# Retention attention and maxout FFN in one kernel: the first weights loaded ahead of block 2, and the first FFN product cut in two halves

## The chip, the cores and the metric

The kernel runs on one core of one Trainium2 chip. The metric is the device time of one execution in microseconds (us), from its first to its last instruction with the little that lies around them; smaller is better.

A core has five engines that run side by side, each through its own queue of instructions in order: TensorE (PE, matmuls; its weight loads are shown as PEld), VectorE (DVE), ScalarE (ACT), GpSimd (POOL) and SyncE (SP), whose queue here issues nearly all transfers. Engines wait for one another, and for transfers, by semaphores.

## The reference

```python
# q, k, v: (8 batches, 8 heads, 576 positions, 64), float32
scores = q @ k.T / sqrt(64)
gamma  = 1 - 2.0 ** (-5 - arange(8))                       # one per head
ret    = scores * where(i >= j, gamma ** (i - j), 0)       # causal, decaying with distance
x      = (ret @ v) -> rows (batch, position), columns (head, dim)   # 4608 x 512
h      = max(x @ w1, x @ w2, x @ w3)                       # w1, w2, w3: 512 x 768
out    = h @ w_out                                         # w_out: 768 x 512, out: 4608 x 512
```

The four weight matrices come as 64-bit floats. [...] the kernel reads them as pairs of 32-bit words and converts them to float32 itself.

## The kernel before

**Blocks.** The 4608 rows are cut into 36 blocks of 128 rows, and four blocks make one FFN tile of 512 rows. For a block the retention is worked out in this way: q and k are transposed on TensorE (`transposes`, L286) and copied from PSUM by ACT (L287); `scores` multiplies them (L300), and DVE multiplies the result with a causal mask into `st`; v is scaled by the decay of its position on POOL (`decay`, L253, giving `vd`); `state` forms k times v for the blocks that follow (`kv`, L366), and `keep` adds it up on DVE and POOL (L372 to L375); `values` multiplies scores and v (`o`, L405), adds the part that comes from the state (L418), and `output` has DVE scale the result into `xT`, the transposed input of the FFN, 128 columns of it for each block. Small DVE steps go through a helper and so stand at L198.

**FFN of the first tile.** Each of the three matrices has six pieces of 128 output columns, and `w_out` has six more; 24 pieces in all. `load_weights(n)` issues the next n pieces from SP, each piece of the three first matrices as two transfers of 256 KB (L502). Six pieces may be under way; a further one is loaded whenever a piece has been converted. `convert(n)` goes n steps further in the conversion of the pieces in their order. A piece takes on DVE two masks (L620, L625), a sum (L631) and two steps of the product (L636, L642, which gives `w`); on ACT one step `mant` (L621) and two steps `expo` (L623, L626). `up_plain` multiplies a piece with the 512 columns of `xT` (L736): four pairs of matmuls. The first result of a piece of columns is copied by ACT (L741), the later ones are combined by a maximum on DVE (L740). For the first product of all, the columns are split in 384 and 128, so that it may begin before block 3's columns are there.

**Order.** Each engine executes in the order in which the program text issues, and this is written out by hand. SP's queue before: k, q, v of block 0; of block 1; state factors `gs`; k, q, v of block 2; k, q of block 3; piece 1; v of block 3; piece 2; k, q, v of block 4; pieces 3 to 6. TensorE's queue before: transposes 0, scores 0, transposes 1, state 0, values 0, scores 1, transposes 2, state 1, values 1, transposes 3, scores 2 and 3, state 2, values 2, values 3 with state 3, then the first FFN product, transposes 4 and the second product. The conversion of piece 1 stands around `values([2])`, that of piece 2 behind `values([3])`. Then `ffn(0)` begins, and the generator `steps(1)` places the retention of blocks 4 to 7 between its products. Later tiles use products with fewer multiplications (L693 to L713); the change leaves them alone.

Of the kernel before, what the change touches and what calls it, by code (L numbers as in the profile page):

```python
# [48 lines left out]
C = 128  # L49
NT = 4 * C  # L50
NH = NT // 2
# [30 lines left out]
def kernel(  # L82
# [23 lines left out]
    CPT = NT // C  # L106
# [68 lines left out]
    def half(j):  # L175
        return slice(D * j, D * (j + 1))
# [5 lines left out]
    late, chores, urgent, scaling, spread = {}, deque(), deque(), deque(), []  # L182
# [42 lines left out]
            vas[g, c] = vpool.tile([P, H, D], FP32, tag=f"va{c}", name=f"va{c}")  # L225
        return vas[g, c]

    def load(g):
        if g >= BY_PE and ("q", g) not in raws:
            load_blocks(g, *range(C // 32))  # L230
        for n, src in (("k", k), ("q", q), ("v", v)) if g < BY_PE else (("k", k), ("v", v)):
            if n == "v" and g == CPT - 1:
                load_weights(1)
            if n == "v" and g >= BY_CHUNKS:
                for c in range(2):
                    b, pos = divmod(g * C + D * c, S)
                    nc.sync.dma_start(stacked(g, c)[half(c)], v[b, :, pos:pos + D, :].rearrange("h p d -> p h d"))
                continue
            bufs = {"k": 3, "q": 2, "v": 4}[n]
            pool, bufs = (raw0, 1) if n != "v" and g < BY_PE and g % (bufs + 1) == bufs else (raw, bufs)  # L240
            if n == "v":
                t = vpool.tile([C, H, D], FP32, tag="va0", name="vraw")
            else:
                t = pool.tile([C, H, D], FP32, tag=n, name=n + "raw", bufs=bufs)
            raws[n, g] = t
            for row, b, pos, m in spans(g):
                nc.sync.dma_start(t[row:row + m], src[b, :, pos:pos + m, :].rearrange("h p d -> p h d"))  # L247
# [19 lines left out]
    def transposes(g):  # L267
        both = qks[g] = {}
        if g >= BY_CHUNKS:
            for n, tag in (("k", "kT"), ("q", "m1")):  # L270
                both[n] = att.tile([P, H, D], FP32, tag=tag, name=tag, bufs=2 if n == "k" else 3)
            ms[g, 0], ms[g, 1] = att.tile([P, H, D], FP32, tag="m0", name="m0"), both["q"]
        else:
            for n in ("k", "q"):
                tag, bufs = ("kT", 2) if n == "k" else (f"m{g % 2}", 3)
                both[n] = att.tile([P, NP, C], FP32, tag=tag, name=n + "T", bufs=bufs)
        if g >= BY_PE:
            for n in ("k", "q"):
                soon(partial(nc.vector.transpose, both[n][:].rearrange("a p c -> a (p c)"),
                             raws.pop(("kx" if n == "k" else n, g))[:].rearrange("a x y i -> a (x y i)")))  # L280
            return
        for n, src in (("k", raws["k", g]), ("q", raws.pop(("q", g)))):
            pool, tag = (ps_r, "r") if g >= CPT else (ps_x, "x")
            pt = pool.tile([P, NP, C], FP32, tag=tag, name=n + "t")
            for p in range(NP):
                nc.tensor.transpose(pt[:, p, :], pair(src, p), ident[:C, :C])  # L286
            nc.scalar.copy(both[n][:], pt[:])  # L287
# [95 lines left out]
    def head(c, n):  # L383

        return NP * c + n
# [104 lines left out]
    def load_weights(n):  # L490
        for _ in range(n):
            if not to_load:
                return
            i, fb = piece = to_load.popleft()
            t = bits[piece] = wraw.tile([P, DM], I64, tag="bits", name="bits")
            if i == "out":
                nc.sync.dma_start(t[:], moe_w_out[fb * P:(fb + 1) * P, :])
            else:
                heads = WS[i][:, fb * P:(fb + 1) * P].rearrange("(h p) f -> p h f", p=D)
                blocks = t[:].rearrange("p (n f) -> p n f", f=P)  # L500
                for c in range(2):
                    nc.sync.dma_start(blocks[half(c)], heads[:, head(c, 0):head(c, NP)])  # L502
# [177 lines left out]
    def convert(n):  # L680
        for _ in range(n):
            next(converting, None)
# [48 lines left out]
    def up_plain(t, h, fb, i):  # L731
        ps = (ps_x, ps_y)[fb % 2].tile([P, NT], FP32, tag="xy"[fb % 2], name="up")
        first_of_all = t == 0 and (fb, i) == (0, 0)
        for cols in (slice(0, NT - C), slice(NT - C, NT)) if first_of_all else (slice(0, NT),):
            for dc in range(NDC):
                nc.tensor.matmul(ps[:, cols], lhsT=w_sb[i, fb][:, dc * P:(dc + 1) * P], rhs=xT[t][:, dc, cols],  # L736
                                 start=dc == 0 and cols.start == 0, stop=dc == NDC - 1,
                                 skip_group_check=first_of_all)
        if i > 0:
            return lambda: nc.vector.tensor_tensor(h[:, fb, :], h[:, fb, :], ps[:], op=ALU.max)  # L740
        return lambda: nc.scalar.copy(h[:, fb, :], ps[:])  # L741

    def ffn(t):

        h = hpool.tile([P, NF, NT], FP32, tag="h", name="h")
        if t == 0:
            for fp, i in units:
                for fb in (2 * fp, 2 * fp + 1):
                    maximum = up_plain(t, h, fb, i)
                    if CPT not in qks:  # L750
                        maximum()
                        transposes(CPT)
                        convert(4)
                        continue
                    convert(4)
                    maximum()
                yield
            convert(6)
            for fb, _ in enumerate(downs_plain(t, h)):
                convert(4 if fb < 2 else 4 * len(pieces))  # L760
                if fb == 2:
                    while_converting.close()
                    late["pool"] = ctx.enter_context(tc.tile_pool(name="late", bufs=1))
                    late_room()
                    sums_of_outs()
                elif fb > 2:
                    chore({3: 4, 4: 0, 5: 2}[fb])
                if fb in (1, 3):
                    yield
            yield  # L770
            return
        if t == 1:
            spread.append(True)
            weight_sums(0)
            weight_sums(2)
        plain = (2, 3) if t == 1 else ()
        order = (2, 3, 0, 1, 4, 5) if t == 1 else (0, 1, 4, 5, 2, 3)
        total = sum(24 if fb in plain else len(PRODUCTS) for fb in order)
        count = parts = 0
        for n, fb in enumerate(order):  # L780
            if fb not in plain:
                while fb // 2 not in summed_fp:
                    chore()
            steps_of_one = up_plain_all(t, h, fb) if fb in plain else up(t, h, fb)
            for step, cost in enumerate(steps_of_one):
                if fb in plain:
                    chore(4 if (fb, step) == (plain[-1], 1) else 8)
                elif step % 2 and (step % 4 == 1 or t == 1 or len(urgent) > 6) or t == 1 and step % 5 == 4:
                    chore(len(urgent) > 0)
                elif step % 4 == 2 and chores:  # L790
                    chores.popleft()()
                if step % 3 == 2:
                    scale()
                count += cost or 1
                if count * (NF // 2 * 3) >= (parts + 1) * total:
                    parts += 1
                    yield
            if n % 2:
                sums_of_hidden(h, fb // 2)
                if fb in plain:  # L800
                    weight_sums(fb // 2)
        chore(len(urgent))
        for n, _ in enumerate(downs(t, h)):
            chore(4)
            scale(2)
            if n in (1, 3):
                yield
        yield
# [8 lines left out]
    for g in range(CPT):  # L817
        load(g)
        if g == 1:
            for j in range(2):  # L820
                nc.sync.dma_start(gs[half(j)], state_decay[half(j), :, half(j)])
    load_weights(1)
    load(CPT)
    load_weights(4)
    decay(0)
    key_masks()
    transposes(0)
# [9 lines left out]
    keep(0)  # L837
    scores(1)
    first_output()
    transposes(2)  # L840
    state_factors()
    decay(2)
    state(1)
    keep(1)
    values([1], [1])
    transposes(3)
    decay(3)
    scores(2)
    scores(3)
    state(2)  # L850
    keep(2)
    convert(2)
    values([2], [2])
    convert(2)
    values([3], [3])
    convert(4)
    keep(3)
    decay(CPT)
    convert(2)

    def steps(t):

# [97 lines left out]
```

## Time and profile before

| | us |
|---|---|
| median of 7 runs | 769.5 |
| lowest and highest | 767.25, 771.82 |
| the profiled execution | 770.87 |
| its span, first to last instruction | 768.9 |

| engine | busy us | share of the span |
|---|---|---|
| PE | 751.3 | 98% |
| PEld | 606.1 | 79% |
| DVE | 588.9 | 77% |
| ACT | 388.9 | 51% |
| POOL | 91.7 | 12% |

The mean granted TensorE clock is 0.998 of full speed. In a row of the profile, `w<-mant,expo` gives what is written and read, `x16` a number of instructions, and "idle before <-releaser" how long the engine stood still ahead of them and what ended it. A busy TensorE is not one at its peak, since matmuls overlap and their ends are modelled; distances from start to start say more.

### The profile page before, as it was taken

The page shows a single profiled execution, that of the slowest core. Times are in us where ns is not written, and L with a number is a line of the kernel's source. Part 1 is how long each engine was busy: PE and PEld are TensorE (multiplying, and loading weights), DVE is VectorE, ACT ScalarE, POOL GpSimd, SP SyncE. Part 2 cuts the span into 40 slices and gives each one's busy share as a digit, 9 for nine tenths or more (in the row PEclk, how much of TensorE's full clock was granted, in tenths as well). Part 3 has the DMA queues.
Part 4 walks back from the last instruction along what each step waited for, and adds up shares of the span by engine and source line. Part 5 has one row for each costly group of instructions (what it writes and reads, how often), then busy time and mean ns, then how long its engine had stood idle before and what let it go on. Part 6 is the DMA issues. An engine that isn't in the chain of part 4 may idle for free.

```text
span 768.9 us, 16109 instructions
## 1 busy us (share of the span) xinstructions
PE 751.3 (98%) x5928; PEld 606.1 (79%) x5928; DVE 588.9 (77%) x1268; ACT 388.9 (51%) x1057; POOL 91.7 (12%) x112
## 2 busy tenths in 40 slices
PE   8999999998999999999999999999999999999998
PEld 7645544686888888888888888878888888888887
DVE  2998998888676867788688959775888678855672
ACT  3574641364256644664466446653666256514651
POOL 3210022102010110011011102010101001100000
PEclk9999999999999999999999999999999999999999
DMA  9995762414041414232243324142415141001001
GB/s 222 221 234 128 186 140 79 87 27 86 28 101 39 79 47 103 51 69 58 68 84 59 66 60 93 30 82 62 80 39 98 42 87 39 2 15 41 1 1 55
DMA packets 230319, 59.40 MB, mean 77 GB/s; under 512 B 211168, under 2 KB 228960, under 8 KB 230240
## 3 DMA queue, kind: packets, MB, share of 16 engines
q1 hardware_dynamic: 229664, 58.04, 35.1%
q8 instruction: 46, 0.75, 0.4%
q10 hardware_dynamic: 576, 0.33, 0.1%
q14 instruction: 33, 0.27, 0.1%
HBM read 48.89 MB, written 9.44 MB: 76 GB/s over the span
## 4 chain that ended last, share of the span: by engine, by line
PE 86%; DVE 9%; SPq 2%; issue 1%; DMA 1%; ACT 1%; DVEq 0%
PE a L713 15%; PE b L713 13%; PE dx L553 11%; PE up L736 11%; PE c L713 6%; PE dz L553 5%; PE d L713 5%; PE e L713 4%; PE o L436 4%; DVE part L693 4%; PE down L723 3%; PE dy L553 3%; DVE m L325 2%; PE sk L317 2%; SPq L247 1%
## 5 line engine op out<-in xcount | busy, mean ns | idle before, releaser
L693 DVE TENSOR_TENSOR part<-part 128x256 f32<-128x256 f32 x460 | 208.3, 462 | 68.7 <-ACT part L698 60.5
L698 ACT COPY part<-a 128x256 f32<-128x256 f32 x276 | 101.8, 369 | 64.6 <-PE a L713 58.6
L698 ACT COPY part<-b 128x256 f32<-128x256 f32 x230 | 85.6, 372 | 86.0 <-PE b L713 81.7
L736 PE MATMUL up<-xT,w 128*128 128x512 f32 (+2 forms) x200 | 84.7, 578 | 1.6 <-DVE w L642 1.6
L713 PE MATMUL a<-s,w 128*128 128x256 f32 x276 | 82.9, 382 | 2.5 <-ACT part L698 2.5
L713 PE MATMUL b<-s,n 128*128 128x256 f32 x276 | 82.1, 379 | 0.0
L736 PEld LDWEIGHTS up<-xT,w 128*128 128x128 f32 x200 | 36.8, 190 | 43.6 <-issue 38.9
L186 ACT ACTIVATE kraw<-kraw,gk 128x64 f32<-128x64 f32 x208 | 66.9, 349 | 0.3
L713 PE MATMUL d<-s,w 128*128 128x256 f32 x184 | 56.7, 390 | 5.4 <-DVE part L693 5.4
L713 PEld LDWEIGHTS a<-s,w 128*128 128x128 f32 x276 | 51.5, 190 | 11.9 <-ACT part L698 3.9
L713 PEld LDWEIGHTS b<-s,n 128*128 128x128 f32 x276 | 52.4, 190 | 7.1
L335 POOL TENSOR_TENSOR va<-va,gs_of 64x512 f32<-64x512 f32 x24 | 26.3, 1097 | 261.7 <-DVE va L333 159.7
L713 PE MATMUL b<-xT,n 128*128 128x256 f32 x184 | 57.3, 394 | 0.0
L713 PE MATMUL c<-xT,w 128*128 128x256 f32 x184 | 54.7, 379 | 0.0
L713 PE MATMUL a<-xT,n 128*128 128x256 f32 x184 | 47.3, 380 | 0.3 <-ACT part L698 0.3
L713 PE MATMUL e<-xT,w 128*128 128x256 f32 x184 | 47.2, 379 | 0.0
L693 DVE TENSOR_TENSOR h<-part 128x256 f32<-128x256 f32 x92 | 40.6, 442 | 6.9
L713 PEld LDWEIGHTS d<-s,w 128*128 128x128 f32 x184 | 34.2, 191 | 14.5 <-DVE part L693 10.1
L325 DVE TENSOR_TENSOR m<-sk,gm 64x512 f32<-64x512 f32 x56 | 38.5, 688 | 8.4 <-PE sk L321 7.2
L553 PE MATMUL dx<-To,H 128*128 128x256 f32 (+1 forms) x204 | 44.9, 370 | 0.0
L560 ACT COPY part<-dx 128x256 f32<-128x256 f32 (+1 forms) x34 | 10.5, 362 | 63.4 <-PE dx L553 61.2
L530 POOL TENSOR_TENSOR H<-h,H 128x256 f32<-128x256 f32 x24 | 18.9, 788 | 188.0 <-DVE H L529 149.0
(121 smaller groups left out, 1372.5 us busy)
## 6 DMA issues: line engine op xcount, KB each, us to landing
bits<-in_moe_w_dram SPq DMA_DIRECT2D x36, 256.0 KB, 5.3
out_dram<-osb SPq DMA_DIRECT2D x35, 256.0 KB, 2.1
kraw<-in_k_dram SPq DMA_DIRECT2D x32, 256.0 KB, 3.1
qraw<-in_q_dram SPq DMA_DIRECT2D x224, 32.0 KB, 2.1
kxraw<-in_k_dram SPq DMA_DIRECT2D x224, 32.0 KB, 2.1
va<-in_v_dram SPq DMA_DIRECT2D x56, 128.0 KB, 3.1
bits<-in_moe_w_out_dram SPq DMA_DIRECT2D x6, 512.0 KB, 6.6
vraw<-in_v_dram SPq DMA_DIRECT2D x7, 256.0 KB, 5.2
```

The lines of the kernel that those rows point to most:

```text
L186: scaling.popleft()()
L317: nc.tensor.matmul(sk[c][half(c), h, :], lhsT=kr[half(c), h, :], rhs=vas[g, c][half(c), h, :], start=True, stop=True)
L325: nc.vector.tensor_tensor(ms[g, c][half(c)], sk[1 - c][half(c)], gm[half(c)], op=ALU.mult)
L335: nc.gpsimd.tensor_tensor(to[half(1)], to[half(1)], gs_of[half(1)].unsqueeze(2).to_broadcast([D, H, D]), op=ALU.mult)
L436: nc.tensor.matmul(o[half(c), n % 2, n // 2, half(m)], lhsT=vas[g, m][:, h, :], rhs=ms[g, m][:, h, :], start=m == 0 and n == 0, stop=True, ...
L530: urgent.append(lambda: (pool(s3, a11, a21, op=ALU.subtract), pool(s4, a12, s2, op=ALU.subtract)))
L553: nc.tensor.matmul(o, lhsT=hS[n](fp)[:, m * P:(m + 1) * P], rhs=late["T"][n][:, fp, cols], start=first and fp == 0 and (m == 0 or last and ...
L693: nc.vector.tensor_tensor(out, a, b, op=op)
L698: nc.scalar.copy(t[:], ps[step[0]][:])
L713: nc.tensor.matmul(ps[chain][:], lhsT=factor(w, fb), rhs=xS[t][x], start=n == 1, stop=ends, skip_group_check=True)
L723: nc.tensor.matmul(b[:], lhsT=h[:, fb, m * P:(m + 1) * P], rhs=w_sb["out", fb], start=(fb == 0), stop=(fb == NF - 1))
L736: nc.tensor.matmul(ps[:, cols], lhsT=w_sb[i, fb][:, dc * P:(dc + 1) * P], rhs=xT[t][:, dc, cols], start=dc == 0 and cols.start == 0, stop= ...
```

## The change

Three things are done. **Loads:** SP's queue gets piece 1 behind the state factors, ahead of block 2, and no longer inside block 3; piece 2 comes behind block 3's v; piece 3 goes between q and v of block 4; then v of block 4 and pieces 4 to 6. **Conversion:** the first two steps of piece 1 go ahead of `values([1])`, the last two behind it; the first two of piece 2 go behind `keep(2)`, its last two behind the copy of the first product's result; `decay(4)` moves there too, and the six steps that follow are those of pieces 3 and 4 that came in part earlier. **First product:** its columns are split in 256 and 256. The first half (blocks 0 and 1) comes behind the transposes of block 3; then `meanwhile` issues scores 3, state 2, keep 2, values 2, values 3 and keep 3; then comes the second half. State 1 moves ahead of the transposes of block 2, scores 2 ahead of those of block 3.

```diff
-    def load(g):
+    def load(g, names="kqv"):
...
-            if n == "v" and g == CPT - 1:
-                load_weights(1)
+            if n not in names:
+                continue
...
-        for cols in (slice(0, NT - C), slice(NT - C, NT)) if first_of_all else (slice(0, NT),):
+        for cols in (slice(0, NH), slice(NH, NT)) if first_of_all else (slice(0, NT),):
+            if cols.start > 0:
+                late.pop("meanwhile")()
...
                     if CPT not in qks:
                         maximum()
+                        convert(2)
+                        decay(CPT)
                         transposes(CPT)
-                        convert(4)
+                        convert(6)
                         continue
...
         if g == 1:
             for j in range(2):
                 nc.sync.dma_start(gs[half(j)], state_decay[half(j), :, half(j)])
+            load_weights(1)
     load_weights(1)
-    load(CPT)
-    load_weights(4)
+    load(CPT, "kq")
+    load_weights(1)
+    load(CPT, "v")
+    load_weights(3)
...
     first_output()
+    state(1)
     transposes(2)
     state_factors()
     decay(2)
-    state(1)
     keep(1)
-    values([1], [1])
+    convert(2)
+    values([1], [])
+    convert(2)
+    scores(2)
     transposes(3)
     decay(3)
-    scores(2)
-    scores(3)
-    state(2)
-    keep(2)
-    convert(2)
-    values([2], [2])
-    convert(2)
-    values([3], [3])
-    convert(4)
-    keep(3)
-    decay(CPT)
-    convert(2)
+
+    def meanwhile():
+        scores(3)
+        state(2)
+        keep(2)
+        convert(2)
+        values([2], [])
+        values([3], [3])
+        keep(3)
+
+    late["meanwhile"] = meanwhile
```

Constants: `C` = 128, `NT` = 512, `NH` = 256, `CPT` = 4.

## The prediction

> **What bounds the kernel now.** I read the page's busy table first, then TensorE's waits, then the timeline of the first 31 us, because everything the change touches happens there.
>
> ```profile
> PE 751.3 (98%) x5928; PEld 606.1 (79%) x5928; DVE 588.9 (77%) x1268; ACT 388.9 (51%) x1057; POOL 91.7 (12%) x112
> ```
>
> TensorE stands still for only about 17 us of 768.9. The start takes 1.4 of them (warm-up matmuls fill the rest until the first block arrives at 4 us); the largest single stall, 3.6 us on DVE, is at 183 us, far from the change. TensorE's waits between 11 and 27 us, which are what the change can fill (columns: us in all, times, longest):
>
> ```profile
> PE up L736 <- DVE w L642: 1.6, 1, 1.6
> PE qt L286 <- DMA qraw<-in_q_dram: 1.4, 2, 1.2
> PE kt L286 <- DMA kraw<-in_k_dram: 0.6, 1, 0.6
> PE o L405 <- POOL vd L253: 0.3, 1, 0.3
> ```
>
> They sum to 3.9 us. In the timeline (start, length, what, idle before it) the places are seen:
>
> ```profile
> 12.24 0.63 PE L286 MATMUL kt<-ident,kraw 128*128 128x128 f32 x4 [0.62 <-DMA kraw<-in_k_dram]
> 13.10 0.63 PE L286 MATMUL qt<-ident,qraw 128*128 128x128 f32 x4 [0.23 <-DMA qraw<-in_q_dram]
> ...
> 17.59 0.63 PE L286 MATMUL qt<-ident,qraw 128*128 128x128 f32 x4 [1.19 <-DMA qraw<-in_q_dram]
> 18.14 2.06 PE L300 MATMUL s<-qT,kT 64*128 64x128 f32 x32
> ...
> 26.37 3.74 PE L736 MATMUL up<-xT,w 128*128 128x384 f32 x16 [1.61 <-DVE w L642]
> 29.95 0.60 PE L286 MATMUL kt<-ident,kraw 128*128 128x128 f32 x4
> 30.39 0.60 PE L286 MATMUL qt<-ident,qraw 128*128 128x128 f32 x4
> 30.82 3.60 PE L736 MATMUL up<-xT,w 128*128 128x512 f32 x8
> ```
>
> The second product starts at 30.82, and from there to 110 us the stage table shows TensorE busy all the time. So **the measure of the change is when that second product starts**; a shift there is passed on whole. DMA is full as well: in this table of stages the last two numbers are the share of the 16 engines and GB/s.
>
> ```profile
> 8.00:12.00 4.00, 3.62 (x56) 2.97 (x55) 1.65 (x4) 1.12 (x2) 2.66 (x3) 1.00 1.14 264
> 12.00:16.00 4.00, 3.53 (x58) 2.84 (x59) 2.50 (x7) 1.56 (x4) 1.73 (x2) 1.00 1.07 246
> ```
>
> Whatever goes to the front of SP's queue therefore pushes what was there.
>
> **What the Trainium skill says.** "TensorE: Matmul & The Clock Gate", on engine queue depths, says ACT and DVE are strict FIFO. The trace agrees: the first product's result is there at about 30.0, and ACT copies it at 32.37, behind two steps of the third piece (30.99 and 31.74) that stand ahead in its queue. "DMA: Bandwidth & Descriptors", section on why a DMA increments its semaphore by 16, says a transfer is spread over up to 16 engines and has landed only when the last has finished. The trace agrees: of the packets between 16 and 17 us only 33 of 283 are of the small kind of q, k and v, so block 3's q was all but moved, yet its transposes start at 17.59. "TensorE: Matmul & The Clock Gate", Part 1, also says that after about 3.4 us idle TensorE's clock is halved. The trace agrees at 183 us: 3.62 us of stall, then a window at 0.55 of the clock:
>
> ```profile
> 183.45:187.07 3.62, 0.00 (x0) 0.00 (x0) 3.42 (x7) 0.42 (x2) 2.01 (x3) 1.00 0.59 128
> 187.07:190.50 3.43, 3.43 (x9) 2.77 (x10) 2.65 (x7) 0.99 (x3) 0.36 (x1) 0.55 0.16 37
> ```
>
> **Part 1: the first piece moves ahead of block 2 on SP.** The piece is two issues of 256 KB (12.90 to 14.65 on SP) that now come before 7.97. Block 2's k landed at 7.97 + 4.1 = 12.1, its q at 8.62 + 4.3 = 12.9, each time confirmed by the transposes 0.1 to 0.2 us later. 524 KB at 250 GB/s are 2.1 us. To this I add a lag: small packets ahead of the piece were late in landing. Block 3's q, next to the piece before, was moved by about 16.0 and landed at 12.13 + 5.3 = 17.4, a lag of 1.4, where k and q of block 2 lag about 0.8; so 0.6 more. q of block 2 then lands at 12.9 + 2.7 = **15.6**. Lower end: v of block 1 landed at 10.45 and q of block 2 2.45 us later, with 2.5 transfers of 256 KB (the state factors count half), 0.98 each; two more make 14.9. Upper end: from k of block 3 (15.0) to v of block 3 (21.4) four transfers, with the piece among them, took 6.4, or 1.6 each; 10.45 + 4.5 x 1.6 = 17.6.
>
> From v of block 3 on the bytes are as before. On SP, two issues of the third piece now precede v of block 4: it lands about 2 us after its 26.3, and its only user, the scaling on POOL (1.22), is wanted by the kv product at 35.4: covered. The eighth piece goes behind block 5's k, q, v, whose buffers are free; before, its conversion came at 46.6 on DVE, and I place its landing at 44.5 (block 5's last issue ends at 39.6 now, two issues or 1.3 us earlier then, and 6.2 to land), still covered. Block 5 lands earlier, which buys nothing: its transposes at 43.03 did not wait.
>
> **Part 2: the conversion of the first piece.** It goes into DVE time that was idle, but its chain hangs on block 2: ACT's queue has both copies of block 2 and the two small factor copies ahead. Measured offsets: q landing 12.92 to the end of the factor copies 14.83, 1.9; on ACT 0.79 + 0.76 + 0.72 = 2.3; on DVE 0.71 + 0.74 = 1.5 to the first matmul. So the first half product starts at 15.6 + 5.7 = **21.3**. TensorE meanwhile does block 2's transposes, block 1's output, scores of block 2 and transposes of block 3, done by about 19.8: it waits 1.5 us for weights again. Scores of block 2 used to run with those of 3, now earlier, and their mask multiply on DVE sits behind the conversion (done by 22.7, wanted at 25).
>
> **Part 3: two halves with blocks 2 and 3 between.** A 256-column pair of matmuls takes 0.43 in the later product rows, so a half is 4 x 0.43 = 1.73 and both 3.46; the old split at 384 took 3.58 (26.37 to 29.95), a gain of 0.1. After the first half, by starts in the timeline: scores of block 3 1.02, kv 0.49, output 2 1.00 + 0.60, output 3 0.93, kv 0.56, state part 0.67: 5.3. They end at 21.3 + 1.7 + 5.3 = 28.3. The second half needs all of block 3's columns, a **new wait**: first of two DVE multiplies, 0.46. Before, 384 columns ran beneath it. The half ends at 28.3 + 0.46 + 1.73 = 30.5, block 4's transposes (0.87) at 31.4. The second piece's last steps are on DVE behind the multiplies: from 28.3, 0.8 + state 0.35 + 0.6 + 0.71 + 0.74 = 3.2, so weights at **31.5**.
>
> The sum: second product at 31.5 against 30.82, **0.7 us later**. As waits: k and q of block 2 grow from 0.85 to about 2.9; 1.19 and 0.28 go; the weights' 1.6 becomes 1.5; 0.46 and 0.1 are new. What was moved is given back, because the transfer ahead delays the block on which its own conversion waits.
>
> Costed at nothing: the third piece's steps on ACT now stand behind the first result's copy and block 4's copies; I get its weights at 36.1 and their use at 36.7, a cover of 0.5, and what exceeds it is paid in full. The scaling of block 4 on POOL moves behind the first result and keeps 4 us. DVE, about 98% busy from 30 to 60, then holds its lead over TensorE, as both shift alike.
>
> The profiled execution took 770.87 (span 768.9), 1.4 over the median 769.5. I predict 769.5 + 0.7 = **770.2**; 0.2%, about what a measurement of this kernel can tell from no change, is 1.5 us.
>
> **The rivals.** *Gain:* block 2 is not delayed, the piece being taken up by slack in DMA. Then q lands at 12.9, the second product starts at 28.8: 767.5. Against it: a share above 1 and 264 GB/s in the stage where the piece would go. Even my lower end of 14.9 only brings zero. A further gain could come from the stall at 183 us and its half clock, if the new alignment shortens it; nothing speaks for that.
> *Slower, block 2 behind the piece:* transfers around it land at 1.6 each, q at 17.6, second product 33.5, +2.7: 772.2. For it: v of block 3 behind the same piece did so. Against it: there the second piece pressed from behind too. It decides from q later than 16.4.
> *Slower, clock:* TensorE stands still from 12.4 until k of block 2 at about 14.8. If that halves the clock for one window of 3.4 us, 1.7 us are lost, of which the 1.5 of waiting for weights hide most: +0.2 to +1.5 over the forecast. The stall of 3.62 brought it on, that of 1.61 did not.
> *Nothing:* the path runs elsewhere and the move doesn't show: 769.5.
>
> **How the numbers follow.** Forecast 0.52 and nothing 0.04, both within 0.2%: same 0.56. Block 2 late 0.26 and clock at its worst 0.07: slower 0.33. Gain 0.11: faster. The range goes from 768.4 (between the gain and no change) to 772.5 (just beyond the late block 2); about one in ten lies outside at each end. The forecast's own range is 769.5 to 771.0 (q at 14.9 to 16.4).
>
> **What would show it.** Right: transposes of block 2 wait over 2 us for k, the half product starts near 21.3 after a wait on DVE's w, a wait of about 0.5 on xT ahead of the second half, second product near 31.5. Wrong: block 2's q landing near 13 (gain) or beyond 16.4; a granted clock below 1 before 20 us; a stall on DVE's w between 31 and 60; a changed stall at 183.

## The result and the profile after

The changed kernel takes 774.89 us (median of 12 runs, 772.10 to 776.39), the kernel before 769.83 (31 runs). The ratio is 1.0064, 95% interval 1.0053 to 1.0075: slower by some 5 us. The forecast was 770.2 with a range to 772.5, so the result lies outside it, on the side to which it gave 0.33. The profiled execution took 776.32 (span 774.5).

The busy table of the changed kernel shows 3.6 us more of busy TensorE for the same instructions, the first hint that some of them ran slower:

```profile
PE 754.9 (97%) x5928; PEld 608.2 (79%) x5928; DVE 588.7 (76%) x1268; ACT 388.9 (50%) x1057; POOL 92.2 (12%) x112
```

TensorE's waits between 11 and 36 us, changed kernel:

```profile
PE kt L286 <- DMA kraw<-in_k_dram: 2.9, 1, 2.9
PE up L738 <- ACT mant L621: 1.5, 1, 1.5
PE up L738 <- DVE w L642: 1.0, 1, 1.0
PE up L738 <- DVE xT L198: 0.5, 1, 0.5
PE qt L286 <- DMA qraw<-in_q_dram: 0.2, 1, 0.2
```

They sum to 6.1 where 3.9 stood before. In this profile the second product is 4.0 later than in the first one of the kernel before (34.87 against 30.82): 2.2 of it are these waits, and about 1.7 is TensorE at half its clock, as shown next. The wait put down to ACT's `mant` is one for the first weights: `mant` was done long ago (17.75 to 18.51), and the matmul starts 0.15 us after DVE has written `w`. The same stretch in the timeline of the changed kernel:

```profile
15.12 0.63 PE L286 MATMUL kt<-ident,kraw 128*128 128x128 f32 x4 [2.87 <-DMA kraw<-in_k_dram]
15.95 0.66 PE L286 MATMUL qt<-ident,qraw 128*128 128x128 f32 x4 [0.21 <-DMA qraw<-in_q_dram]
16.54 1.98 PE L405 MATMUL o<-st,vd 128*64 128x128 f32 x16
18.45 1.13 PE L418 MATMUL o<-qT,state 64*64 64x128 f32 x16
...
23.29 1.97 PE L738 MATMUL up<-xT,w 128*128 128x256 f32 x8 [1.46 <-ACT mant L621]
...
31.03 1.99 PE L738 MATMUL up<-xT,w 128*128 128x256 f32 x8 [0.51 <-DVE xT L198]
...
34.87 3.70 PE L738 MATMUL up<-xT,w 128*128 128x512 f32 x8 [0.97 <-DVE w L642]
```

The second product starts at 34.87 instead of 30.82. Block 1's output (L405, 16.54 to 18.45) takes 1.91 us from start to start; it took 0.97 before. The stage table of the changed kernel says why: the third number from the end is the granted clock.

```profile
12.00:16.00 4.00, 0.92 (x15) 0.60 (x10) 2.61 (x7) 0.16 (x1) 0.00 (x0) 1.00 0.96 205
16.41:19.83 3.42, 3.42 (x36) 2.63 (x36) 0.22 (x1) 3.04 (x7) 1.74 (x2) 0.50 1.08 264
```

TensorE was busy 0.92 of 4 us, and after that it had half its clock for 3.42 us, so some 1.7 us of work were lost. What follows on DVE decides how much of that comes through. DVE's queue in the changed kernel, around the first piece's weights, and POOL beside it:

```profile
19.61 0.76 DVE L198 TENSOR_TENSOR xT<-o,gq 128x256 f32<-128x256 f32 x2 [5.00 <-PE o L418]
20.28 0.68 DVE L631 SCALAR_TENSOR_TENSOR mant<-frac,mant 128x512 f32<-128x512 int32 x1
20.88 1.53 DVE L636 SCALAR_TENSOR_TENSOR expo<-bits,expo 128x512 int32<-128x512 int32 x1
22.45 0.69 DVE L642 TENSOR_TENSOR w<-mant,expo 128x512 f32<-128x512 f32 x1
```

```profile
20.72 1.15 POOL L253 TENSOR_TENSOR vd<-vraw,gk 128x512 f32<-128x512 f32 x1 [2.21 <-DMA vraw<-in_v_dram]
```

The last three steps of the conversion stand in the queue behind `xT` of block 1, and `xT` waits for the output that the half clock delays. ACT had finished its part of the piece at 19.88, but the DVE step that uses it (L636) began only at 20.88. It then took 1.53 instead of 0.68, with POOL's scaling of block 3 running beside it.

**Which base.** A second profile of the kernel before, in the first experiment below, took 769.81, which is its median; the first profile (770.87) was 1 us above. In the second one, the second product starts at 30.05, 19.77 us behind the start of scores 1 (10.28); in the first the distance was 20.37. Since traces begin a little apart, I compare this distance and take 19.77 as base. The changed kernel has 24.41, in a second profile 24.53: by then 4.6 to 4.8 us are lost, or 4.0 to 4.2 against the first profile. Each distance comes from one execution, and the two of the kernel before are 0.6 apart, so a difference of that size between two kernels is weak where no second pair repeats it.

### The profile page after: what moved, and what is told of

The parts are those of the page before. It is cut to its first block, busy times and chain, and to the rows that moved or that the text cites. A ratio compares the mean times of both kernels' runs of the same rounds, so it can differ in the third digit from the quotient of the medians.

```text
span 774.5 us, 16108 instructions
## 1 busy us (share of the span) xinstructions
PE 754.9 (97%) x5928; PEld 608.2 (79%) x5928; DVE 588.7 (76%) x1268; ACT 388.9 (50%) x1057; POOL 92.2 (12%) x112
## 4 chain that ended last, share of the span: by engine, by line
PE 85%; DVE 10%; SPq 2%; issue 1%; DMA 1%; ACT 1%; DVEq 0%
PE a L713 15%; PE b L713 13%; PE dx L553 11%; PE up L738 11%; PE c L713 6%; PE dz L553 5%; PE d L713 5%; DVE part L693 4%; PE e L713 4%; PE o L436 3%; PE down L723 3%; PE dy L553 3%; DVE m L325 3%; PE sk L317 2%; DVE h L693 1%; DVE va L333 1%
## 5 line engine op out<-in xcount | busy, mean ns | idle before, releaser
L738 PE MATMUL up<-xT,w 128*128 128x512 f32 (+1 forms) x200 | 85.0, 579 | 2.9 <-ACT mant L621 1.5
L698 ACT COPY part<-d 128x256 f32<-128x256 f32 x92 | 34.3, 373 | 14.1 <-PE d L713 10.1
```

What stands on the lines that cost most here:

```text
L698: nc.scalar.copy(t[:], ps[step[0]][:])
```

## The experiments

Each was run beside the kernel before. "Distance" is that from the start of scores 1 to the start of the second product, in one profiled execution; medians and ratios are of all the runs of a comparison on one chip.

| kernel | distance us | median us, before beside it | ratio and 95% interval |
|---|---|---|---|
| before, second profile | 19.77 | 769.81 (one run), 770.0 | |
| changed, again | 24.53 | 774.83, 769.77 | 1.0057 (1.0039 to 1.0075) |
| loads only | 22.48 | 772.19, 769.40 | 1.0036 (1.0024 to 1.0048) |
| loads only, dummies | 21.11 | 771.47, 769.65 | 1.0024 (1.0014 to 1.0033) |
| order only | 27.75 | 778.03, 769.40 | 1.0112 (1.0094 to 1.0130) |
| whole first product | 21.62 | 771.78, 769.40 | 1.0032 (1.0019 to 1.0045) |
| whole first product, dummies | 20.62 | 771.26, 769.77 | 1.0016 (1.0007 to 1.0025) |
| changed, dummies | 22.42 | 773.29, 769.40 | 1.0060 (1.0038 to 1.0081) |
| changed, scaling early | 23.66 | 773.31, 770.0 | 1.0043 (1.0027 to 1.0060) |
| changed, both (first form) | 24.29 | 775.15, 770.0 | 1.0071 (1.0056 to 1.0086) |
| changed, both (second form) | 22.42 | 773.46, 769.77 | 1.0048 (1.0035 to 1.0060) |
| masks early | 18.17 | 769.54, 770.0 | 0.9993 (0.9981 to 1.0005) |

**Base and repetition.** Both kernels unchanged.

> The kernel before, unchanged, for a second profile. The first profiled execution was 770.87, 1.1 to 1.4 over the median, so one of two things holds. If its beginning was late, the second product stands here 1 us or more earlier behind scores 1 than the 20.4 us of the first profile, and the true loss at the second product is nearer 5 than 4 us. If its beginning was typical, that distance is 20.4 +- 0.2 again, and a shorter span comes from later stages.

The distance is 19.77, a little over half of the 1 us that the first branch asked for; the base was late by 0.6.

> The changed kernel, unchanged, on the same chip as the two others, for a fair base and a second profile. Theory A': wait of 2 to 3 us for block 2's k, clock halved for one window that begins between 15 and 18 us, block 1's output 1.8 to 2 us long; second product 24.2 to 24.8 behind scores 1; median 4 to 5.5 above the kernel before. Rival (the halved clock was a chance of one execution): no halved clock before 20 us in this profile.

The wait for k was 1.96, that for q another 1.68, and the half clock came again (0.67 of the clock from 16 to 18, 0.50 from 18 to 20). It was no chance of one execution.

**The clock.** The changed kernel with nine 128x128 matmuls in the wait, whose result nobody reads (`warm` is given the pool to write to):

```diff
     state(1)
+    warm(9, ps_x, "x")
     transposes(2)
```

> The changed kernel with nine dummy 128x128 matmuls on TensorE in the wait for block 2's k (nothing else differs). Theory A (the stall of 2.87 us halves TensorE's clock from 16.4 to 19.8, and that is over a fourth of the loss): no halved clock before 20 us, block 1's output 1.0 instead of 1.9 us, first half product near 22.0 instead of 23.3, second product 33.5 instead of 34.9; median some 1.4 us under the changed kernel, 773.5. Theory B (the clock is a by-stander, since TensorE waits for the first weights afterwards anyway): the half product starts within 0.3 us of 23.3, median 774.5 to 775.2.

The timeline of this kernel:

```profile
11.72 2.27 PE L150 MATMUL warm<-ident 128*128 128x128 f32 x18
14.00 0.63 PE L286 MATMUL kt<-ident,kraw 128*128 128x128 f32 x4
15.33 0.63 PE L286 MATMUL qt<-ident,qraw 128*128 128x128 f32 x4 [0.71 <-DMA qraw<-in_q_dram]
15.89 1.09 PE L405 MATMUL o<-st,vd 128*64 128x128 f32 x16
...
20.84 1.97 PE L738 MATMUL up<-xT,w 128*128 128x256 f32 x8 [1.14 <-DVE w L642]
...
32.43 3.70 PE L738 MATMUL up<-xT,w 128*128 128x512 f32 x8 [0.98 <-DVE w L642]
```

The clock stays at 1.00, the output of block 1 takes 1.02, and the distance falls from 24.41 to 22.42: 2.0 us, more than theory A said. In this execution the last two steps of the first weights also were free of POOL (0.69 each), so some 0.8 of the 2.0 is POOL's and about 1.2 the clock's. The median, 773.29, lies 3.9 above the kernel before instead of 5.1, and the two intervals overlap: in the time itself this run alone doesn't show a gain.

**One part alone.** Loads of the changed kernel in the kernel before (`load` too is the changed one):

```diff
             for j in range(2):
                 nc.sync.dma_start(gs[half(j)], state_decay[half(j), :, half(j)])
+            load_weights(1)
     load_weights(1)
-    load(CPT)
-    load_weights(4)
+    load(CPT, "kq")
+    load_weights(1)
+    load(CPT, "v")
+    load_weights(3)
```

> The kernel before with the changed order of loads alone. Theory A (loads carry the loss: block 2 lands 2.9 us later, the clock is halved): wait of about 2.9 us for k, clock halved between 16 and 20, second product 2 to 3 us later than 30.8; median 772 to 773.5. Theory C (the split product and the conversion between outputs carry the loss, the loads cost at most what the forecast said): second product within 0.8 us of 30.8, median within 1 us of 769.8.

Theory A held: k waits 2.96, clock at 0.50 from 16 to 18, distance 22.48. The loads alone cost 2.7 in the distance and 2.8 in the median. With dummies, eleven here:

```diff
     first_output()
+    warm(11, ps_x, "x")
     transposes(2)
```

> The kernel before with the changed order of loads alone, as in the run with loads only, and eleven dummy matmuls in the wait for block 2's k. Theory A' (of the 2.1 to 2.7 us which the loads alone cost, over half is the halved clock; the late block itself is mostly taken up by the waits for block 3's q and for its v, which go): no halved clock before 20 us, block 1's output 1.0 instead of 1.9, second product 20.8 to 21.4 us behind scores 1 (22.5 with loads only, 19.8 and 20.4 before); median 0.8 to 1.8 above the kernel before. Rival (the late block costs its full 2 us by itself): second product at 22 or later, median 2.5 or more above.

The clock stayed at 1.00 and the distance is 21.11: 1.4 of the 2.7 was the half clock, 1.3 the late block itself.

The order of the changed kernel with the loads of before (and `load` as it was):

```diff
-            load_weights(1)
     load_weights(1)
-    load(CPT, "kq")
-    load_weights(1)
-    load(CPT, "v")
-    load_weights(3)
+    load(CPT)
+    load_weights(4)
```

> The changed order of work with the old order of loads. Block 2 is in time (transposes near 12.2), but the first piece lands at 19.8 and its steps on ACT stand ahead of block 3's copies. Theory A: TensorE waits 4 to 6 us for the first weights from about 18, the half product starts near 23.5, and the clock is halved after it; second product near 35.5 to 36.5, median 774.5 to 777. Theory D (the early loads alone lose, the new order is harmless): second product within 1 us of 30.8, median within 1 us of 769.8.

```profile
23.72 3.75 PE L738 MATMUL up<-xT,w 128*128 128x256 f32 x8 [5.35 <-DVE w L642]
```

The half product waits 5.35 us for weights and then takes 3.7 instead of 1.9, at half clock. Slower still than expected: without the early load this order is worse than with it, so the two parts aren't two separate losses.

**The cut product.** Changed kernel, the first product in one place behind block 3:

```diff
-        for cols in (slice(0, NH), slice(NH, NT)) if first_of_all else (slice(0, NT),):
-            if cols.start > 0:
-                late.pop("meanwhile")()
+        for cols in (slice(0, NT - C), slice(NT - C, NT)) if first_of_all else (slice(0, NT),):
-    late["meanwhile"] = meanwhile
+    meanwhile()
```

> The changed kernel, but scores 3 to keep 3 are issued ahead of the first product, which is split 384 and 128 as before; loads and conversions stay as changed. Theory A: TensorE no longer waits for the first weights at 21.8; scores 3 follow at once, the first product starts near 28 and the second near 33; median 1.5 to 2 us under the changed kernel, 773. Theory C (halves are right, other parts lose): second product at 34.9 or later, median at or above 774.9.

Distance 21.62, median 771.78: without the halves the change loses half as much, though the clock is halved here too (0.60 from 16 to 18, 0.55 from 18 to 20). With the line `warm(9, ps_x, "x")` besides:

> Changed loads and early conversion, first product in one place behind block 3 (384 and 128), and nine dummy matmuls in the wait for k. Theory A' (with the clock kept, loading first costs the 2 us of block 2 and the early weights give 1.6 back, no more): second product 20.1 to 20.7 us behind scores 1, where the kernel before has 19.8 to 20.4 and the same kernel without dummies 21.6; median 0 to 1 above the kernel before. Rival (the gap between the whole and the halved product was the clock too): second product at 21.4 or later, median 1.5 or more above.

20.62, as theory A' had it for the distance; the median is 1.5 above the kernel before, at the edge of the rival. So loading and converting the first piece early, with the clock kept, brings nothing over the kernel before.

The cut itself costs 1.8 in the distance with the clock kept (20.62 to 22.42) and 2.8 at half clock (21.62 to 24.41). In the medians with the clock kept it is 2.4: 1.5 and 3.9 above the kernel before, and the two intervals don't meet. The traces show where it goes. The whole product starts without a wait:

```profile
26.77 3.74 PE L736 MATMUL up<-xT,w 128*128 128x384 f32 x16
```

In the changed kernel with dummies TensorE waits 1.14 for the first weights, 0.52 for block 3's columns and 0.98 for the second piece's weights; the kernel with the whole product has two waits around block 3's scores in their place, 0.73 and 0.70. That is 1.2 of the 1.8; 0.3 is an earlier start of block 2's q there (5.05 behind scores 1 instead of 5.32).

**POOL beside DVE.** Block 4's scaling issued ahead of scores 3:

```diff
                         convert(2)
-                        decay(CPT)
                         transposes(CPT)
                         convert(6)
...
     def meanwhile():
+        decay(CPT)
         scores(3)
```

> The changed kernel with block 4's scaling on POOL issued ahead of scores 3 instead of behind the first product's result. Theory A' (POOL beside DVE stretches the last two steps of the second piece, 1.22 and 1.41 instead of 0.69 each, and TensorE's 0.97 us wait comes of it): w of the second piece back to about 0.7, that wait 0.3 or less, second product 0.6 to 0.9 earlier than in the changed kernel; median about 774.2. Rival (the steps are late since they stand behind block 3's multiplies, whatever POOL does): the wait stays at 0.8 or more, median 774.5 to 775.3.

In the changed kernel, the last step of the second piece's conversion and POOL's work beside it:

```profile
33.41 1.41 DVE L642 TENSOR_TENSOR w<-mant,expo 128x512 f32<-128x512 f32 x1
```

```profile
31.72 1.11 POOL L375 TENSOR_TENSOR state<-state,gs 128x256 f32<-128x256 f32 x1 [2.80 <-DVE state L374]
32.78 1.49 POOL L253 TENSOR_TENSOR vd<-vraw,gk 128x512 f32<-128x512 f32 x1
```

With the scaling moved away, the same step:

```profile
33.33 0.69 DVE L642 TENSOR_TENSOR w<-mant,expo 128x512 f32<-128x512 f32 x1
```

TensorE's wait falls from 0.97 to 0.25 and the distance by 0.75. The two engines did slow each other. (The step ahead of it, 1.22 long, stays so: POOL's work on the state still runs beside it.)

Both remedies together, the two diffs above, scaling ahead of scores 3 and dummies:

> The changed kernel with both the nine dummy matmuls in the wait for k and block 4's scaling issued early. Theory A': both effects add, second product 1.9 +- 0.4 less 0.7 late behind scores 1 against the kernel before, so 21.4 to 22.0 us after scores 1 start instead of 24.4; median 772.4 to 773. What is left then is the load moved ahead of block 2 and the wait for block 3's columns. Rival (other parts lose as well): median stays at 773.3 or more, as with the dummy matmuls alone.

A failure that teaches something else. In this kernel's timeline:

```profile
30.66 0.67 PE L418 MATMUL o<-qT,state 64*64 64x128 f32 x16 [1.72 <-POOL state L375]
```

POOL's queue stood at the scaling until v of block 4 landed (28.89), and the state for output 3 was queued behind it (29.89). In the second form the scaling stands behind `keep(2)`:

```diff
     def meanwhile():
-        decay(CPT)
         scores(3)
         state(2)
         keep(2)
+        decay(CPT)
```

> As with dummy matmuls and early scaling together, but block 4's scaling stands behind keep 2 on POOL instead of ahead of it, so that the state of block 3 is not held up behind a transfer. Theory A': no wait of output 3 for the state, second piece's last step 0.7 instead of 1.4, second product 21.5 to 21.9 us behind the start of scores 1 (changed kernel 24.4, with the dummies alone 22.4); median 2.3 to 3 under the changed kernel of the same call. Rival (the two losses are not independent, or a later stage takes them back): less than 1.5 under it.

That wait is gone, and the second piece's wait is 0.25, yet the distance is 22.42, the same as with dummies alone:

```profile
21.91 1.97 PE L738 MATMUL up<-xT,w 128*128 128x256 f32 x8 [1.86 <-DVE w L642]
```

Here block 3's scaling on POOL (19.79 to 21.22) fell on the first piece's last step, which began at 20.36 and took 1.41; with dummies alone the scaling began at 20.31, 0.31 into that step, which still took 0.69. What one overlap gave, another took: the expected 21.5 to 21.9 was missed by that 0.7. Against the kernel with early scaling alone, which had a like overlap (a step of 1.53; 23.66), the dummies bring 1.24: the clock's share again. TensorE's wait for the first weights is 1.86 here and 1.39 there, so of the 1.7 that the half clock takes this wait hid about 0.5.

**What the change was after, without moving a transfer.** In the kernel before, DVE's steps are put in another order and the product is cut in its old place:

```diff
-        for cols in (slice(0, NT - C), slice(NT - C, NT)) if first_of_all else (slice(0, NT),):
+        for cols in (slice(0, NH), slice(NH, NT)) if first_of_all else (slice(0, NT),):
...
     scores(2)
+    convert(2)
     scores(3)
     state(2)
     keep(2)
     convert(2)
     values([2], [2])
-    convert(2)
     values([3], [3])
```

> The kernel before with its loads; DVE's first two steps of the first piece go between the mask multiplies of blocks 2 and 3 and the last two ahead of block 2's output, and the first product is split 256 and 256 in its old place. Theory A (what the change wanted can be had on DVE alone: no transfer moves, TensorE has no new idle): the weights' wait of 1.6 shrinks to 0.3 or less, second product about 1.2 earlier, median 0.8 to 1.2 under the kernel before. Rival (the mask multiply of block 3 comes later and holds up output 3, or the second half waits for block 3's columns): second product within 0.4 us of before, median the same.

The weights' wait fell from 1.6 to 0.6 and the distance to 18.17, of which some is an earlier landing of block 3's q in this execution. Both fall short of theory A: the median is only 0.5 below the kernel before, with an interval that holds 1. No version is shown to beat it.

## Why the prediction was wrong

In the distance, the changed kernel's loss can be built up in steps, each a difference of two runs: early loads with the clock kept +1.3 (19.77 to 21.11), early conversion -0.5 (20.62), the cut product +1.8 (22.42), the dummies taken away, so that the clock halves, +2.0 to 2.1 (24.41, 24.53). The sum is 4.6 to 4.8. In the medians the same steps are +1.8, -0.3, +2.4 and +1.2, together 5.1. Not all of the last step is the clock: pairs that differ in it alone, or nearly, give 1.0 (21.62 to 20.62, whole product), 1.4 (22.48 to 21.11, loads only) and 1.2 (23.66 to 22.42, early scaling). The rest of it is a DVE step that POOL stretched in the first profile, and a later landing of q in the second. Of the cut product's 1.8, 0.75 is block 4's scaling on POOL.

- **The steps that failed are the two chains of Part 2 and Part 3 that end on DVE.** From the landing of q to the first half product 5.7 us were put, and 7.5 were measured (15.8 to 23.29); from the end of output 3 to the second piece's weights 3.2, and 4.3 were measured. With 0.2 for q and 0.2 for what lies between, these two make up the 3.4 between the forecast 31.5 and the measured 34.87. Part 2 was added up with TensorE at full clock and with nothing beside DVE. In the changed kernel the half clock made DVE start its last two steps 1.0 late (20.88, where ACT was through at 19.88), and POOL made one of them 0.84 longer. With the dummies, where neither came in, the same chain took 5.6 (15.24 to 20.84), as forecast. In Part 3 the clock was full again, and two DVE steps took 1.22 and 1.41 beside POOL where 0.71 and 0.74 were put. So POOL beside DVE, for which nothing was put, has about 2 us of the 3.4, and the clock about 1.
- **The measure** (second product) was right as far as the stall on DVE in the 180s: TensorE doesn't wait between the two, and both kernels have that stall (3.6 and 3.5). Behind it the two profiles of the changed kernel lose 1.5 to 1.8 more (see what stays open).
- **Part 1** was right. q of block 2 was put at 15.6; it was issued at 9.92 and took 5.9, so 15.8. The wait for k was forecast as over 2, and is 2.87; in the second profile it was 1.96, with 1.68 for q.
- **The rival "Slower, clock"** came about, and it had chance 0.07. The half clock came in both profiles, and in those of the three other kernels that had the early load and no dummies; the five with dummies had full clock up to 20 us. Its cost was put at 0.2 to 1.5 over the forecast, and the runs give 1.0 to 1.4. So the size was right at its upper end, and by itself it would have stayed inside the range (770.2 + 1.5 = 771.7). What failed is its chance and its argument that the 1.5 us of waiting for weights would hide most of the 1.7: they hid 0.2 to 0.5 (1.14 with dummies against 0.98 in the second profile of the changed kernel, 1.86 against 1.39 in the pair with early scaling). That wait isn't fixed: DVE takes its steps in order, the first piece's sum stands behind `xT` of block 1, and that waits for TensorE's slowed output. `xT` started at 19.61, with the dummies at 17.62, and the weights moved along. I had named the in-order queues and not looked whether the hidden work itself hung on the slowed engine.
- **The stall that halves the clock** was bounded by two cases of the trace before, 1.61 (no) and 3.62 (yes). The Trainium skill ("TensorE: Matmul & The Clock Gate", Part 1) names an idle window of about 3.4 us. Taken as waits of TensorE, shorter ones were enough here: 2.25 with 0.61 behind it (whole first product), 1.96 with 1.68 (changed, again). But between and behind these waits only the transposes of block 2 ran. From the last other matmul ahead of them to the next one it is 4.29 us in the changed kernel (12.25 to 16.54) and 3.5 to 5.3 in all five profiles with the early load and no dummies; the eight profiles with full clock between 9 and 36 us have no such gap above 2.9. So either shorter waits suffice, or transposes don't count as work for the clock. No run here tells the two apart.
- **Part 3** was right in its new wait (0.51 for 0.46). The halves took 1.89 and 1.83 from start to start, not 1.73. Its last term was mis-sized: weights of the second piece 3.2 us behind the end of output 3; measured 4.3, as said above.
- **"The scaling of block 4 on POOL ... keeps 4 us"**: its user indeed didn't wait. But I asked only who waits for POOL, not who works beside it. The Trainium skill ("GPSIMD Engine Reference", Key points) says GpSimd shares its SBUF interfaces with VectorE, with contention for DVE instructions with two SBUF inputs; the 1.41 against 0.69 agrees.
- **The rival "Slower, block 2 behind the piece"** did not come about in the first profile: q at 15.8, not 17.6. In the second, q landed at 16.54, about the 16.4 from which this rival was to be taken; the distance there was only 0.12 longer.
- **The base**: the first profile's start of the second product was 0.6 later than that of the median execution. A profile 1 us above its median has that somewhere. The forecast of 770.2 added a shift against the late profile to a median, and so was 0.6 too low by this alone.

**What stays open.** How much of the loss in the time itself is the clock can be estimated from the times of all runs too. At a mean granted clock of 0.995 or 0.996 the changed kernel takes 774.5 (median of 8 runs) and the kernel before 770.65 (26 runs), 3.9 apart. At 1.000 the changed kernel has only two runs, 772.10 and 771.99, where the kernel before has a median of 767.4 (six runs). So some 4 of the 5.1 us are there at equal clock, and about 1 is the clock's; the mean doesn't say where in a run the slow windows lay.

For the changed kernel with dummies, with and without early scaling, the medians lie 3.7 and 3.9 above the kernel before, where the distances say 2.65. Executions differ in how many windows of 3.4 us they spend at half clock: one takes 0.0022 from the mean (3.4 / 2 / 774), and the changed kernel's runs have 0.993 to 1.000, those of the kernel before 0.995 to 1.000. Behind the late stall the changed kernel had two such windows in both profiles, as the table of stages shows, where both profiles before had one:

```profile
190.00:194.00 4.00, 2.77 (x7) 2.24 (x8) 3.74 (x10) 0.62 (x2) 0.75 (x2) 0.56 0.58 131
194.00:198.00 4.00, 4.00 (x13) 3.22 (x12) 2.41 (x7) 1.74 (x5) 0.00 (x0) 0.58 0.00 0
```

Whether that is an effect of the shift or chance wasn't tried; some experiments had one, others two.

## What to carry to other kernels

Ahead of a transfer that TensorE waits for, put nothing whose own use hangs on that transfer: the early weights were converted behind the very block that they delayed. A product cut in two begins earlier, but it gives up the cover under which weights and columns came in: here three waits appeared. A new stall of TensorE is to be priced with the slower clock that may follow it, and slack hides that in full only if the work which it waits for doesn't itself hang on TensorE. When a step is moved on POOL, look at what DVE does at that time, and at what stands behind it in POOL's own queue, not only at who waits for its result.

## What the runs showed of the hardware

Dummy matmuls in a wait of 2 to 3 us, nine (2.3 us long) or eleven (2.7), went with full clock up to 36 us in each of the five profiles in which they ran. POOL and DVE slow each other: a DVE step on 128x512 floats in SBUF went from 0.69 to 1.41 and POOL's scaling from 1.04 to as much as 1.57 (early scaling, 20.23) when they met, and DVE's masking of integers that read one tensor also went from 0.42 to 0.96 beside POOL's state factor (28.24 in the changed kernel). After a wait of 5.35 us the clock came back only 5.7 us into the work that followed (order only: 0.50 from 23.72 to 29.40, 1.00 from there to 32).
